# Two spectral layers side by side on one core: from a scheduled instruction order to one written out for every queue

## The chip, the cores and the metric

One core of one Trainium2 chip runs the kernel. The core has five queues of its own: TensorE (PE, with its weight loads as PEld), VectorE (DVE), ScalarE (ACT), GpSimd (POOL) and SyncE (SP), and 16 DMA engines that all queues feed. The metric is device time in microseconds of one launch; lower is better.

## The reference

Inputs: `A_x` and `B_x` of 1 x 2048 x 512, filters `A_w_r`, `A_w_i` of 2048 x 257, and four DFT matrices for B, two of 2048 x 2048 and two of 512 x 512, all float32. The output is 1 x 2048 x 1024, A's 512 columns beside B's.

```python
def _A_ref(x, w_r, w_i):                 # A_x, A_w_r, A_w_i
    B, S, D = x.shape
    X = jnp.fft.rfft2(x, axes=(-2, -1))
    X = X * (w_r + 1j * w_i)
    return jnp.fft.irfft2(X, s=(S, D), axes=(-2, -1))

def _B_ref(x, dft_seq_re, dft_seq_im, dft_hid_re, dft_hid_im):
    a = jnp.einsum("bsd,ed->bse", x, dft_hid_re)
    b = jnp.einsum("bsd,ed->bse", x, dft_hid_im)
    return jnp.einsum("ts,bse->bte", dft_seq_re, a) - jnp.einsum("ts,bse->bte", dft_seq_im, b)

return jnp.concatenate([a, b], axis=-1)
```

## The kernel before

Three strands of work share the engines; each is a Python generator in one function (`tile_concat_...`, line 209).

**A** (`a_work`, 423) is a factored two-dimensional FFT. `forward` (284) takes eight groups of input rows, two to a block: DVE folds a block (`TT`, 228), PE multiplies by the hidden-dimension table (`hid`, line 296), ACT copies the result out of PSUM (298), PE applies a 16-point step along the sequence (301), ACT copies again (303), and two DMAs per group, issued by ACT (306), put the result into the tile `zv` with the partition dimension rearranged. These are the *turns*: 16 of 256 KB, each with a source of 128 partitions and a destination of 8. `slot` (311) then works on `zv` in eight parts ("slots", in the order `SLOTS`): load of the filter part `w` and of a table `fi` (316, 322), a patch of one column of `w` by GpSimd (317), DVE sums (328 to 333), a forward matmul (338, or 341 for slot 0), the product with the filter on DVE (2048 elements per partition in one instruction), four DVE sums that combine its parts, an inverse matmul (382, 385), and two ACT copies back into `zv` (387). `inverse` (392) needs all of `zv`: for each of eight halves of a quarter, PE (406), an ACT copy (408), PE (412), an ACT copy (414), two DVE sums, and for each quarter a store of 1 MiB to `out_a` by SP (419).

**B** (`b_work`, 458) is the same kind of factored transform of `B_x`. Four blocks of 1 MiB are loaded (464 to 471), ACT makes a reversed copy `xr` (478, 479), PE transforms 16 groups (485, 486; "al" below), ACT gathers them into `yall` (488). Then for nine row sets `hidden` (497 to 503) and for eight `rows_of` (516 on): PE, an ACT copy with two halves (525), two DVE sums, a reversed ACT copy (528), a plain row store issued by ACT (509) and a scatter of mirrored rows issued by GpSimd (512). `yb`, which they leave from, has two buffers.

**C** (`c_work`, 565) makes the factored transform of B legitimate: it loads all of B's four DFT matrices, 34 MiB in 34 blocks of 1 MiB, and compares them with tables (`unequal`, 563) on DVE, counting differences in `stat`. At the end the counts are summed into `flag`, every engine loads the flag (621) and branches (622) around `_b_from_c`, which computes B from the matrices as given and is not run with these inputs. The sign of a table's odd columns is changed by ACT between its two uses (574, 595).

A's input blocks, B's input blocks and C's blocks share one set of six 1 MiB buffers (`block`, `NB = 6`). PSUM has three two-bank tiles for A (`ps_a`) and two one-bank tiles for B (`ps_b`).

The order: `ORDER` says how the three generators are stepped while the program is traced,

```python
ORDER = "a9 b8 a60 b20 c"
```

but that is only the order of tracing. The context is opened with `schedule_with_timeline_sim=True`, and its scheduler places each instruction on its engine's queue by dependences, free buffers and its own idea of when an instruction becomes ready. On the chip each queue then runs strictly in the order it was given, and waits on semaphores.

Of the kernel before, what the change touches and what calls it, by code (L numbers as in the profile page):

```python
# [16 lines left out]
P = 128  # L17
# [5 lines left out]
ORDER = "a9 b8 a60 b20 c"  # L23
# [102 lines left out]
def _tables():  # L126
# [54 lines left out]
    for h in range(2):  # L181
# [16 lines left out]
        "ht": ht.astype(np.float32),  # L198
# [3 lines left out]
        "mb": mb.astype(np.float32),  # L202
        "hc": hc.astype(np.float32),
        "turn": turn.astype(np.int32),
    }


@with_exitstack
def kernel(
# [15 lines left out]
    last = [None]  # L225

    def TT(**kw):
        last[0] = nc.vector.tensor_tensor(**kw)  # L228

    mm = nc.tensor.matmul  # L230
# [5 lines left out]
    ps_a = first.enter_context(tc.tile_pool(name="ps_a", bufs=3, space=PSUM))  # L236

# [6 lines left out]
    def block():  # L244
        return sp.tile([P, 2048], F32, name="blk", bufs=NB)

    load = nc.sync.dma_start

    ones = const("ones", P)
    nc.vector.memset(ones, 1.0)  # L250
    zero = sp.tile([P, 512], mybir.dt.bfloat16, name="zero")
    nc.vector.memset(zero, 0.0)
    warm = ps_a.tile([P, 2, 512], F32, name="pa")
    for _ in range(9):
        mm(warm[:, 0], zero[:, :P], zero, start=True, stop=True)

# [10 lines left out]
    tf = const("ta", 1152, src=tabs["first"], by=nc.scalar)  # L267
    hf = tf[:, :1024].rearrange("p (k h f) -> p k h f", k=2, h=2)
    f16 = tf[:, 1024:]
    wsp_sb = const("wsp_sb", 8, 2, 2, 2, src=wsp, by=nc.gpsimd)  # L270
    odd = const("odd", 2, src=tabs["odd"], by=nc.gpsimd)
    sgn = const("sgn", 2, 2)
    nc.gpsimd.memset(sgn[:, 0], 1.0)
    nc.gpsimd.memset(sgn[:, 1], -1.0)
    we = const("we", 8, 2, 2)

    xs = []
    for b in range(4):
        t = block().rearrange("p (c r f) -> p c r f", c=2, r=2)
        for c in range(2):  # L280
            load(t[:, c].rearrange("p r (k f) -> p r k f", k=2), xa[0, :, 2 * b + c])
        xs.append(t)

    def forward():
        for b in range(4):
            u = part(2048 * (b % 2), 2, 2, 2, 256)
            for h, op in enumerate((ADD, SUB)):
                TT(out=u[:, h].rearrange("p c k f -> p c (k f)"), in0=xs[b][:, :, 0], in1=xs[b][:, :, 1], op=op)
            for c in range(2):
                i = 2 * b + c  # L290
                pd = ps_a.tile([P, 2, 512], F32, name="pa")
                for r in range(2):
                    for h in range(2):
                        out = pd[:, r].rearrange("p (q h f) -> p h q f", q=2, h=2)[:, h]
                        for k in range(2):
                            mm(out, u[:, h, c, k, 128 * r : 128 * r + 128], hf[:, k, h], start=k == 0, stop=k == 1)  # L296
                zs = part(4096 + 1024 * (i % 2), 2, 512)
                nc.scalar.copy(zs, pd)  # L298
                y = ps_a.tile([P, 2, 512], F32, name="pa")
                for r in range(2):  # L300
                    mm(y[:, r], f16, zs[:, r], start=True, stop=True)  # L301
                ys = part(6144 + 1024 * (i % 2), 2, 512)
                nc.scalar.copy(ys, y)
                for r in range(2):
                    at = _place(8 * r + i, 0)
                    nc.scalar.dma_start(zv[at : at + 29 : 4], ys[:, r])
                yield

    def slot(e, n):

        z = zv[:, 2 * e : 2 * e + 2].rearrange("p r (q h f) -> p r q h f", q=2, h=2)
        w = sp.tile([P, 2, 2, 2, 128], F32, name="w", bufs=3)
        for h in range(2):
            load(w[:, :, :, h], wa[h, e])
        nc.gpsimd.tensor_copy(w[:, :, :, 0, 0], we[:, e].rearrange("p f r -> p r f"))  # L317
        t = part(1024 * (n % 3), 2, 2, 2, 128)
        tab = tabs["fi"].rearrange("p (e i f) -> p e i f", e=11, i=2)
        if e:  # L320
            fi = sp.tile([P, 1, 2, 128], F32, name="fi", bufs=4)
            load(fi, tab[:, e - 1 : e])
        else:
            fi = const("fi0", 4, 2, 128, src=tab[:, 7:], by=nc.sync)
        ft, it = fi[:, :, 0], fi[:, :, 1]

        def flat(v):
            return v.rearrange("p q h f -> p (q h f)")

        if e:  # L330
            TT(out=t[:, 0], in0=z[:, 1], in1=z[:, 0, ::-1], op=ADD)
            TT(out=t[:, 1], in0=z[:, 0], in1=z[:, 1, ::-1], op=SUB)
            nc.vector.tensor_copy(t[:, :, :, 0, 0], z[:, :, :, 0, 0])  # L333
        yield
        px = ps_a.tile([P, 2, 2, 2, 128], F32, name="pa")
        for i in range(2):
            if e:
                mm(flat(px[:, i]), ft[:, 0], flat(t[:, i]), start=True, stop=True)  # L338
            else:
                for j in range(2):  # L340
                    mm(flat(px[:, i]), ft[:, 2 * i + j], flat(z[:, j]), start=j == 0, stop=j == 1)
        yield
        x = px
        if e == 0:
            x = t
            g = part(7168, 2, 2, 128)
            nc.scalar.copy(g, px[:, 1])
            TT(out=x[:, 0], in0=px[:, 0, ::-1], in1=g, op=ADD)
            TT(out=x[:, 1], in0=px[:, 0], in1=g[:, ::-1], op=SUB)
            nc.scalar.copy(x[:, :, :, 0, 0], px[:, :, :, 0, 0])  # L350
# [12 lines left out]
        TT(out=m1[:, 1:3], in0=m1[:, 1:3], in1=m2[:, 3::-3], op=SUB)
        y = m1.rearrange("p (r q) (h f) -> p r q h f", r=2, h=2)

        yo = t
        TT(out=yo[:, 0], in0=y[:, ::-1, 0], in1=y[:, :, 1], op=ADD)
        TT(out=yo[:, 1], in0=y[:, 1, ::-1], in1=y[:, 0], op=SUB)
        TT(out=yo[:, :, :, 0, 0], in0=y[:, :, :, 0, 0], in1=sgn, op=MUL)
        if e == 0:  # L370
            nc.scalar.copy(yo[0:1, 0], y[0:1, ::-1, 0])
            nc.scalar.mul(yo[0:1, 1], y[0:1, :, 1], -1.0)
            nc.scalar.copy(yo[0:1, 0, :, 0, 0], cn[:, 0])
            nc.scalar.mul(yo[0:1, 1, :, 0, 0], cn[:, 1], -1.0)
        yield

        pi = ps_a.tile([P, 2, 4, 128], F32, name="pa")
        for i in range(2):
            for q in range(4):
                lhs = [yo[:, k].rearrange("p q h f -> p (q h) f")[:, q] for k in range(2)]  # L380
                if e:
                    mm(pi[:, i, q], lhs[i], it[:, 0], start=True, stop=True)  # L382
                else:
                    for k in range(2):
                        mm(pi[:, i, q], lhs[k], it[:, 2 * k + i], start=k == 0, stop=k == 1)
        for i in range(2):
            nc.scalar.copy(zv[:, 2 * e + i].rearrange("p (n q g) -> p n q g", n=8, q=4),  # L387
                           pi[:, i].rearrange("p q (n g) -> p n q g", n=8))

    def inverse():

        tl = const("ta", 1152, src=tabs["late"], by=nc.sync)
        di = tl[:, :1024].rearrange("p (h q n) -> p h q n", h=2, q=2)
        g16 = tl[:, 1024:]
        gz = zv.rearrange("p k f -> p (k f)")
        for quad in range(4):
            ob = part(3072 + 2048 * (quad % 2), 2, 2, 4, 128)
            for half in range(2):  # L400
# [9 lines left out]
                for j in range(2):  # L410
                    for q in range(4):
                        mm(po[:, j, q // 2, q % 2], u[:, j, q], g16, start=True, stop=True)  # L412
# [327 lines left out]
```

## Time and profile before

| | |
|---|---|
| time, median of 3 runs | 319.95 us (318.28 to 321.04) |
| the profiled execution | 320.22 us, its span 318.4 us |
| mean granted TensorE clock | 0.821 |
| busy, us: PE, PEld, DVE, ACT, POOL | 201.8, 149.8, 152.5, 72.5, 28.0 |
| moved by DMA | 70.35 MB, mean 221 GB/s |
| of it read from HBM, written to it | 57.54 MB, 8.39 MB |

The span is the time from the first instruction to the last of one profiled execution; its own time has 1.8 us more around it. Busy time counts compute instructions only. A matmul of float32 stands as two records. The slices cut the span into 40 parts of 8 us, with the busy share of each in tenths. In the list of stages a row has the stretch, then for each engine its busy time and its count of instructions, then the granted clock of TensorE, the mean busy share of the 16 DMA engines (which can be a little over 1, as packets overlap) and GB/s. A releaser after `<-` is what ended an engine's idle time.

### The profile page before, as it was taken

To read this page: it belongs to the slowest core of one execution; us is meant where nothing else is said; L and a number is where in the kernel's file an instruction comes from. 1 tells how busy PE (TensorE), PEld (TensorE's weight loads), DVE (VectorE), ACT (ScalarE), POOL (GpSimd) and SP (SyncE) were. 2 spreads that over 40 slices of the span, in tenths; PEclk is the share of its full clock that TensorE was granted. 3 is DMA by queue.
4 is the path that set the end of the run, shared out by engine and by line. 5 is a ranking of instruction groups with operands and counts; after the bars stand their busy time and mean duration, and the time that the engine had idled before them with its cause. 6 is when DMAs were issued, how large, how long until landed. Compare 5 with 4: busy or idle time off the path is not lost.

```text
span 318.4 us, 2428 instructions
## 1 busy us (share of the span) xinstructions
PE 201.8 (63%) x849; PEld 149.8 (47%) x849; DVE 152.5 (48%) x199; ACT 72.5 (23%) x114; POOL 28.0 (9%) x25
## 2 busy tenths in 40 slices
PE   5760049999989524948088200797927688788850
PEld 1540018888876312523065000473525587688850
DVE  0520000560275541499999999986694211111220
ACT  1010014424452212400014100423302122322220
POOL 2000000000000000100050079011120000000000
PEclk9995559999999975695659855597877799999995
DMA  7999999663999999799999997032210000230303
GB/s 269 391 288 291 213 279 342 241 249 94 397 334 340 338 300 350 271 360 401 404 308 358 389 333 308 35 126 89 99 66 33 2 0 31 100 134 0 132 3 139
DMA packets 30002, 70.35 MB, mean 221 GB/s; under 512 B 1936, under 2 KB 11024, under 8 KB 29472
## 3 DMA queue, kind: packets, MB, share of 16 engines
q1 hardware_dynamic: 25760, 61.12, 56.6%
q10 hardware_dynamic: 3488, 6.88, 6.2%
q0 software_dynamic: 736, 2.14, 1.7%
q8 instruction: 8, 0.13, 0.2%
q14 instruction: 10, 0.08, 0.1%
HBM read 57.54 MB, written 8.39 MB: 207 GB/s over the span
## 4 chain that ended last, share of the span: by engine, by line
PE 39%; DMA 28%; DVE 18%; ACT 5%; issue 5%; SPq 3%; ACTq 0%; DVEq 0%
DMA blk<-in_cm 13%; DVE work L228 11%; PE pa L406 9%; DMA blk<-in_xb 8%; DVE blk L563 6%; PE pa L412 5%; PE pa L296 4%; DMA zv<-work 4%; PE pa L382 4%; PE pa L338 3%; PE pa L301 3%; ACT work L408 3%; DMA blk<-in_xa 2%; PE pb L485 2%; PE pb L501 2%
## 5 line engine op out<-in xcount | busy, mean ns | idle before, releaser
L563 DVE SCALAR_TENSOR_TENSOR blk<-blk,tt 128x2048 f32<-128x2048 f32 (+2 forms) x24 | 41.6, 1754 | 25.8 <-DMA blk<-in_cm 18.2
L563 DVE SCALAR_TENSOR_TENSOR blk<-blk,odd,tt 128x2048 f32<-128x2048 f32 x16 | 37.2, 2346 | 5.4 <-DMA blk<-in_cm 5.4
L497 PE MATMUL pb<-hc,yall 128*128 128x257 f32 x18 | 8.0, 536 | 46.4 <-DVE work L228 33.1
L228 DVE TENSOR_TENSOR work<-pa,work 128x512 f32<-128x512 f32 x18 | 11.6, 685 | 51.3 <-ACT work L414 51.3
L296 PE MATMUL pa<-ta,work 128*128 128x256 f32 x128 | 31.2, 400 | 3.9 <-DVE work L228 3.9
L301 PE MATMUL pa<-work,ta 128*128 128x512 f32 x32 | 17.1, 660 | 24.8 <-ACT work L298 24.8
L296 PEld LDWEIGHTS pa<-ta,work 128*128 128x128 f32 x128 | 25.9, 203 | 11.7 <-DVE work L228 4.8
L406 PE MATMUL pa<-ta,zv 128*128 128x256 f32 x128 | 30.5, 391 | 1.2 <-ACT zv L387 1.2
L228 DVE TENSOR_TENSOR work<-blk 128x1024 f32<-128x1024 f32 x8 | 9.4, 1222 | 43.4 <-PE pa L296 42.9
L406 PEld LDWEIGHTS pa<-ta,zv 128*128 128x128 f32 x128 | 28.8, 304 | 1.5 <-ACT zv L387 1.5
L497 PEld LDWEIGHTS pb<-hc,yall 128*128 128x128 f32 x18 | 3.7, 244 | 51.7 <-issue 35.3
L382 PE MATMUL pa<-fi,work 128*128 128x128 f32 x112 | 18.1, 328 | 10.4 <-DVE work L228 10.4
L512 POOL DMA_INDIRECT out_b<-yb,turn x8 | 13.4, 1678 | 117.9 <-DMA out_b<-yb 112.9
L382 PEld LDWEIGHTS pa<-fi,work 128*128 128x128 f32 x112 | 17.6, 241 | 12.7 <-issue 12.5
L412 PE MATMUL pa<-ta,work 128*128 128x128 f32 x128 | 16.4, 281 | 9.1 <-ACT work L408 9.1
L338 PE MATMUL pa<-work,fi 128*128 128x512 f32 x28 | 18.2, 793 | 5.5 <-DVE work L333 4.4
L317 POOL COPY w<-we 128x4 f32<-128x4 f32 x8 | 12.5, 1571 | 92.0 <-DMA w<-in_wa 87.2
L412 PEld LDWEIGHTS pa<-ta,work 128*128 128x128 f32 x128 | 14.9, 191 | 11.5 <-ACT work L408 11.5
L298 ACT COPY work<-pa 128x1024 f32<-128x1024 f32 x8 | 8.1, 1013 | 53.2 <-PE pa L296 29.4
L301 PEld LDWEIGHTS pa<-work,ta 128*128 128x128 f32 x32 | 6.0, 206 | 30.2 <-ACT work L298 25.8
L228 DVE TENSOR_TENSOR work<-work 128x512 f32<-128x512 f32 x32 | 20.1, 680 | 0.1
L228 DVE TENSOR_TENSOR work<-pa,w 128x2048 f32<-128x2048 f32 x7 | 15.9, 2284 | 8.4 <-PE pa L338 8.4
(72 smaller groups left out, 232.3 us busy)
## 6 DMA issues: line engine op xcount, KB each, us to landing
blk<-in_cm SPq DMA_DIRECT2D x32, 1024.0 KB, 7.1
tt<-tab_tt SPq DMA_DIRECT2D x4, 1026.0 KB
blk<-in_xa SPq DMA_DIRECT2D x8, 512.0 KB, 6.7
w<-in_wa SPq DMA_DIRECT2D x16, 256.0 KB, 7.1
zv<-work ACTq DMA_DIRECT2D x16, 256.0 KB
out_a<-work SPq DMA_DIRECT2D x4, 1024.0 KB, 4.1
blk<-in_xb SPq DMA_DIRECT2D x7, 512.0 KB
blk<-in_wd SPq DMA_DIRECT2D x2, 1024.0 KB
```

The lines of the kernel that those rows point to most:

```text
L228: last[0] = nc.vector.tensor_tensor(**kw)
L296: mm(out, u[:, h, c, k, 128 * r : 128 * r + 128], hf[:, k, h], start=k == 0, stop=k == 1)
L301: mm(y[:, r], f16, zs[:, r], start=True, stop=True)
L317: nc.gpsimd.tensor_copy(w[:, :, :, 0, 0], we[:, e].rearrange("p f r -> p r f"))
L338: mm(flat(px[:, i]), ft[:, 0], flat(t[:, i]), start=True, stop=True)
L382: mm(pi[:, i, q], lhs[i], it[:, 0], start=True, stop=True)
L406: mm(pu[:, j, h], gz[:, 32 * q + 16 * h + g :: 64], di[:, h, q], start=q == 0, stop=q == 1)
L408: nc.scalar.copy(u, pu.rearrange("p j h (k n) -> p j (h k) n", k=2))
L412: mm(po[:, j, q // 2, q % 2], u[:, j, q], g16, start=True, stop=True)
L497: mm(out, yall[:, a0], hc[:, 0], start=True, stop=False)
L512: nc.gpsimd.indirect_dma_start(out=out_b, out_offset=bass.IndirectOffsetOnAxis(ap=turn[:, o : o + 1], axis=0), in_=v, in_offset=None)
L563: nc.vector.scalar_tensor_tensor(raw, raw, k, v, op0=MUL, op1=ALU.not_equal, accum_out=stat[:, i : i + 1])
```

## The change

The generators are taken apart into some 400 named steps, each of which issues instructions on one engine only. The string `PLAN` lists the steps; they are traced in that order, and every instruction is tied behind the one traced before it on the same engine, so that the scheduler cannot move it. A step's name is a kind and a number: `xa` A's loads, `fold`, `hid`, `zs`, `f16_`, `ys` and `tu` the parts of `forward`, `w`, `fix`, `sf`, `fwd`, `prod`, `comb`, `inv`, `ev` those of a slot (with `g`, `sx`, `spec`, `spy` for slot 0), `late`, `hi`, `eu`, `g16_`, `sc`, `eo`, `st` those of `inverse`; `xb`, `xr`, `al`, `av`, `bh`, `hv`, `ro`, `y1`, `y2`, `y3`, `pt` (and `rx`, `ry`) B's; `tt`, `cl`, `sg`, `cc` the tables, loads, sign changes and comparisons of C, where 16 and 17 are those of the hidden matrices.

Beside the order these things change:

- A's first four input groups are loaded one by one and folded half by half for the first block; the later ones come one block per load. The runs in memory are longer.
- The part of a slot is laid out with the width half `h` ahead of the rest. The filter's two loads per slot become one with longer runs, and its product becomes two DVE instructions of 1024 elements.
- The tables `hc`, `ht` and `mb` are one tile `bt`, loaded at once.
- The turns, B's plain row stores, the late table and the stores to `out_a` are issued from GpSimd's queue; before, ACT issued the first two and SP the others.

```diff
-ORDER = "a9 b8 a60 b20 c"
+PLAN = """
+xa0 we xa1 xa2 xa3 xa5 xa7 tt0 tt1 bt fold0 cl0 fold1 hid0 cl1 fb fold3 hid1 zs0 w0 f16_0 zs1 fold5 hid2 ys0
+tu0 w1 f16_1 zs2 hid3 ys1 tu1 w2 cc0 f16_2 zs3 fold7 hid4 xb0 cc1 cl2 fix0 f16_3 zs4 ys2 hid5 tu2 xb1 cl3 fix1
+ys3 tu3 f16_4 zs5 cl4 fix2 cl5 hid6 xr0 f16_5 zs6 cc2 al0 ys4 al1 av0 tu4 hid7 av1 cc3 f16_6 zs7 ys5 al2 sg4
+tu5 f16_7 av2 cc4 al3 late cl6 av3 cc5 cl7 xr1 ys6 al4 ys7 tu6 al5 av4 tu7 al6 av5 cc6 al7 av6 cl8 av7 cl9 xb2
+xb3 cc7 fwd2 sf0 sf1 tt2 cc8 cl10 cc9 fwd0 g2 fwd1 prod0 cl11 xr2 cl12 al8 prod1 w3 al9 cl13 av8 al10 av9
+comb0 w4 al11 av10 av11 cl14 comb1 xr3 al12 sx2 al13 av12 cc10 al14 spec2 av13 inv0 av14 prod2 fix3 inv1 ev0
+sf3 w5 al15 ev1 comb2 fwd3 cl15 av15 cl16 fix4 bh8 prod3 spy inv2 hv8 sf4 w6 fix5 comb3 fwd4 ev2 sf5 inv3
+prod4 bh0 ev3 sf6 fix6 w7 fwd5 comb4 hv0 ro0 prod5 fix7 inv4 y10 y20 comb5 bh1 y30 ev4 rx sf7 hv1 fwd6 ry cc11
+pt0 ro1 bh2 y11 prod6 cl17 sg12 inv5 hv2 y21 comb6 y31 ro2 ev5 pt1 bh3 y12 cc12 inv6 hv3 y22 cl18 fwd7 ev6
+cc13 y32 ro3 pt2 bh4 prod7 y13 cl19 y23 hv4 comb7 ro4 y33 pt3 bh5 y14 cc14 inv7 hv5 y24 cl20 ev7 cc15 ro5 y34
+bh6 y15 pt4 cc16 tt3 cl21 hi0 hv6 y25 cl22 sg17 y35 cc17 pt5 ro6 eu0 bh7 y16 tt4 cl23 y26 y36 g16_0 cc18 hv7
+pt6 ro7 sc0 hi1 cc19 cl24 eo0 cl25 hi2 cc20 eu1 y17 y27 cl26 cc21 y37 g16_1 eu2 pt7 g16_2 cl27 sg22 sc1 cc22
+hi3 sc2 eo1 cl28 eo2 st0 hi4 eu3 cc23 cc24 cl29 g16_3 eu4 g16_4 sc3 cc25 cl30 hi5 sc4 eo3 cl31 cc26 st1 hi6
+eu5 cc27 cl32 eo4 cl33 eu6 cc28 g16_5 g16_6 sc5 cc29 hi7 sc6 eo5 sg30 cc30 st2 eu7 cc31 g16_7 eo6 sc7 eo7 cc32
+st3 cc33
+"""
...
+class _InOrder:
+
+    def __init__(self, tc, engine):
+        self._tc, self._engine = tc, engine
+
+    def __getattr__(self, name):
+        def issue(*args, **kwargs):
+            return self._tc.keep_in_program_order(getattr(self._engine, name)(*args, **kwargs))
+        return issue
...
+    pe, dve, act, pool, sync = (_InOrder(tc, e) for e in (nc.tensor, nc.vector, nc.scalar, nc.gpsimd, nc.sync))
+    mm, TT, load = pe.matmul, dve.tensor_tensor, sync.dma_start
...
+        @step(f"ys{i}")
+        def _():
+            act.copy(ys, flat(at["py", i]))
+
+        @step(f"tu{i}")
+        def _():
+            for r in range(2):
+                lo = _place(8 * r + i, 0)
+                pool.dma_start(zv[lo : lo + 29 : 4], ys[:, r])
...
-        w = sp.tile([P, 2, 2, 2, 128], F32, name="w", bufs=3)
-        for h in range(2):
-            load(w[:, :, :, h], wa[h, e])
...
+        @step(f"w{n}")
+        def _():
+            w = at["w", n] = sp.tile([P, 2, 2, 2, 128], F32, name="w", bufs=3)
+            load(w, wa[:, e].rearrange("h p i q f -> p h i q f"))
...
+        @step(f"prod{n}")
+        def _():
+            x, w = at["px", n] if e else t, at["w", n]
+            for h in range(2):
+                x2 = x[:, h].rearrange("p r q f -> p r (q f)").unsqueeze(1).to_broadcast([P, 2, 2, 256])
+                w2 = w[:, h].rearrange("p i q f -> p i (q f)").unsqueeze(2).to_broadcast([P, 2, 2, 256])
+                TT(out=m[:, h].rearrange("p i (r q) f -> p i r (q f)", r=2), in0=x2, in1=w2, op=MUL)
...
+    @step("late")
+    def _():
+        tl = const("ta", 1152, src=tabs["late"], by=pool)
...
+            @step(f"st{quad}")
+            def _():
+                pool.dma_start(out_a.rearrange("(r p) s -> p r s", p=P)[:, :, 512 * quad : 512 * quad + 512],
+                               ob.rearrange("p r k g s -> p (r k) (g s)"))
...
+        @step(f"pt{o}")
+        def _():
+            y = at["y", o]
             if o:
-                put(rows[o], y[:, 0])
-                put_turned(o, y[:, 1])
...
+                pool.dma_start(rows[o], y[:, 0])
...
+            pool.indirect_dma_start(out=out_b, out_offset=bass.IndirectOffsetOnAxis(ap=turn[:, o : o + 1], axis=0),
+                                    in_=y[:, 1], in_offset=None)
...
+    for name in PLAN.split():
+        steps.pop(name)()
+    assert not steps, steps
```

More of the change, by code (lines that the diff above doesn't have):

```diff
@@ L251, with part @@
     zero = sp.tile([P, 512], mybir.dt.bfloat16, name="zero")
[L252 to L255, printed above, removed]
+    dve.memset(zero, 0.0)
     zv = const("zv", 16, 512)
     work = const("work", 8192)
-    def part(at, *shape):
-        v = work[:, at : at + math.prod(shape)]
+    def part(lo, *shape):
+        v = work[:, lo : lo + math.prod(shape)]
         names = "abcde"[: len(shape)]
@@ L272 @@
+    odd = const("odd", 2, src=tabs["odd"], by=pool)
+    turn = sp.tile([P, 8], mybir.dt.int32, name="turn")
+    pool.dma_start(turn, tabs["turn"])
     sgn = const("sgn", 2, 2)
-    nc.gpsimd.memset(sgn[:, 0], 1.0)
-    nc.gpsimd.memset(sgn[:, 1], -1.0)
+    pool.memset(sgn[:, 0], 1.0)
+    pool.memset(sgn[:, 1], -1.0)
     we = const("we", 8, 2, 2)
[L277 to L292, printed above, removed]
-                    for h in range(2):
[L294 to L307, printed above, removed]
@@ L425, in a_work, with _ @@
+    for i in range(8):
+        forward(i)
+    @step("we")
+    def _():
         TT(out=we[:, :, :, 0], in0=wsp_sb[:, :, :, 0, 0], in1=wsp_sb[:, :, :, 1, 0], op=ADD)
@@ L427, in a_work @@
         TT(out=we[:, :, 1, 1], in0=wsp_sb[:, :, 1, 0, 1], in1=wsp_sb[:, :, 1, 1, 1], op=SUB)
-        gens = [slot(e, n) for n, e in enumerate(SLOTS)]
-        def stage(n):
-            if 0 <= n < 8:
-                next(gens[n], None)
-        stage(0)
-        stage(0)
-        stage(1)
-        yield
-        for n in range(9):
-            stage(n)
-            yield
-            stage(n - 1)
-            stage(n + 1)
-            yield
-            stage(n + 2)
-            yield
-        yield from inverse()
@@ L495, in hidden, with _ @@
+        for g in range(4):
+            group(g)
+    for q in range(4):
+        along(q)
+    m_b = mb[:, :1408].rearrange("p (k f) -> p k f", f=128)
+    rows = out_b.rearrange("(c e) d -> e c d", e=16)
+    def hidden(e):
+        @step(f"bh{e}")
+        def _():
+            bank = bank_b(("bh", e))
             a0, a1, a2 = (0, 7, 7) if e == 8 else (1 + e, 8 + e, e - 1 if e else 8)
@@ L606, with compare, four, _ @@
[L606 to L613 removed]
+        dve.scalar_tensor_tensor(raw, raw, k, v, op0=MUL, op1=ALU.not_equal, accum_out=stat[:, i : i + 1])
+    def compare(i, k, q, mt, half, tb):
+        raw = "c", i
+        def four(name):
+            return at[name].rearrange("p (j c) -> p j c", j=4)
+        @step(f"cl{i}")
+        def _():
+            lo = 4 * half + 2 * q
+            block(raw)
+            load(four(raw).rearrange("p (r j) c -> p r j c", r=2), cm[mt, tb, lo : lo + 2].rearrange("r p j c -> p r j c"))
+        if half and tb == 0:
+            @step(f"sg{i}")
+            def _():
+                act.mul(at["t", k][:, :, 1::2], at["t", k][:, :, 1::2], -1.0)
+        @step(f"cc{i}")
+        def _():
+            t = at["t", k]
+            neg = int(tb % 2 == 1 and mt == 1)
+            unequal(i - 2 * (i > 15), four(raw), t[:, :, 512:0:-1] if tb % 2 else t[:, :, :512],
+                    odd[:, neg : neg + 1] if tb in (1, 2) else (-TINY if neg else TINY))
```

544 lines of the change are left out of this document (303 added, 241 removed).

## Prediction

> **What bounds the kernel now.** I read the slices of the page first: they show when each engine works.
>
> ```profile
> PE   5760049999989524948088200797927688788850
> DVE  0520000560275541499999999986694211111220
> DMA  7999999663999999799999997032210000230303
> ```
>
> DMA is full until about 200 us (25 slices of 8 us) and then almost idle; PE has holes early and in the middle and is dense only at the end, when VectorE (DVE) and DMA have nothing left. The three busy resources stand one behind the other. The stages, by columns PE, PEld, DVE, ACT, POOL (busy us), granted clock, DMA share, GB/s:
>
> ```profile
> 28.00:43.00 15.00, 0.00 (x0) 0.00 (x0) 0.00 (x0) 0.00 (x0) 0.00 (x0) 0.50 1.05 215
> 79.00:118.00 39.00, 29.55 (x138) 22.23 (x136) 19.26 (x19) 12.89 (x20) 0.00 (x0) 0.97 1.02 348
> 118.00:134.00 16.00, 9.90 (x20) 5.79 (x21) 4.27 (x5) 4.67 (x8) 0.00 (x0) 0.53 0.87 311
> 134.00:201.00 67.00, 27.79 (x81) 15.34 (x79) 66.20 (x91) 10.10 (x18) 19.89 (x7) 0.70 0.93 348
> 182.00:201.00 19.00, 0.00 (x0) 0.00 (x0) 18.97 (x23) 1.32 (x2) 13.87 (x3) 0.50 0.85 302
> 201.00:253.00 52.00, 38.66 (x156) 26.65 (x156) 35.17 (x51) 13.91 (x28) 5.48 (x6) 0.77 0.18 64
> 253.00:310.00 57.00, 45.74 (x256) 43.17 (x256) 10.15 (x16) 13.00 (x17) 0.00 (x0) 1.00 0.15 56
> ```
>
> From 253 on the whole inverse of A runs alone: 57 us with DVE busy 10 and DMA at 15%. At 28 to 43 PE stands still. Why, the ACT timeline says, and the chain of waits shows the inverse's period:
>
> ```profile
> 43.12 1.01 ACT L298 COPY work<-pa 128x1024 f32<-128x1024 f32 x1 [23.88 <-DMA blk<-in_xb]
> ...
> 257.22 1.02 ACT work L408
> ...
> 258.28 2.05 PE pa L412 x16
> 260.33 3.65 PE pa L406 x16
> ```
>
> ACT's next copy of A stood 23.88 us behind a load for B: an order of queues, not a lack of data. In the inverse PE pays 2.05 + 3.65 us and waits for the copy L408 between them.
>
> **The change: the sums that no order can beat.** Bytes and arithmetic stay, but for longer runs in the loads of A's input and weights. Totals of the page:
>
> ```profile
> PE 201.8 (63%) x849; PEld 149.8 (47%) x849; DVE 152.5 (48%) x199; ACT 72.5 (23%) x114; POOL 28.0 (9%) x25
> ...
> q1 hardware_dynamic: 25760, 61.12, 56.6%
> q10 hardware_dynamic: 3488, 6.88, 6.2%
> ...
> core 0: 318.4 us, clock 0.821
> ```
>
> DMA: 56.6 + 6.2% of 318.4 us is 200 us, with the 2% of the small queues 206. PE: 201.8 x 0.821 = 165.7 us of work at full clock. DVE: 152.5 us. So the written order can bring the span near DMA's 206 us if everything lies beside the loads; I walk it in three stages.
>
> **Stage 1, to the last input block of B (xb3).** SP's written order puts before it, in MiB: first table 0.56, xa 4, tt0 and tt1 2, bt 1.44, ten comparison blocks (cl0 to cl9) 10, fb 0.39, three slots' weights and tables 2.25; GpSimd adds the turns 4 and late 0.56: 25.2, and xb itself 4.
>
> ```profile
> blk<-in_cm SPq DMA_DIRECT2D x32, 1024.0 KB, 7.1
> ...
> 1.67 7.43 DMA blk<-in_xa
> ```
>
> At 348 GB/s (row 79:118, loads and turns together) a MiB costs 3.01 us; in 28:43, where xb was the load, 215 GB/s gives 4.88. So 25.2 x 3.01 + 4 x 4.88 = 95.4 us; with 1.7 us to the first byte, xb3 lands at **97 us**. What PE has to do in it, what a turn's issue takes, and how long rows of B (yb) take to land:
>
> ```profile
> 9.24 5.86 PE L296 MATMUL pa<-ta,work 128*128 128x256 f32 x16 [3.88 <-DVE work L228]
> ...
> 47.92 3.45 PE pa L296 x16
> ...
> 53.70 1.72 PE pa L301 x4
> ...
> L306 ACTq DMA_DIRECT2D zv<-work x16: 622/624/1224, 37.5 to 122.4; - x16
> ...
> DMA to landing us min/median/max: 2.7/2.8/6.9
> ```
>
> From 9 us on, 8 x (3.45 + 1.72) = 41 us of forward work: half of the stage. So the engines wait for landings, and the written order adds waits: DVE's cc7 (for cl7) stands ahead of sf0; ACT's xr0 and xr1 (for xb0, xb1) stand ahead of copies of A, with PE's hid7 and f16_6 behind them; on GpSimd fix0 waits for the load w0 with the turns tu2 and on behind it, and ys4 on ACT waits for tu2's landing. All of these loads stand ahead of xb3 on SP, so the waits end before it and cost nothing as long as the loads are the last; if they aren't, that is the second rival below. The three loads hc, ht, mb become one and ACT loses 16 turn issues: hidden here too, and without that cover worth what SP's and ACT's issues take, about 0.6 us each.
>
> **Stage 2, to the last product's end (comb7).** PE's order puts inv0 behind al14, so behind xb3. Rows:
>
> ```profile
> L479 ACT COPY xr<-blk x4: 1043/1043/1044, 49.0 to 87.5; 128x1020 f32<-128x1020 f32 x4
> ...
> 96.71 0.34 PE pb L485 x2
> ...
> 97.39 0.24 PE pb L485 x2
> ...
> 226.65 1.78 PE pa L382 x16
> ```
>
> xr3 1.2, three groups al12 to al14 of 4 such pieces (2 x 0.34 + 2 x 0.24 = 1.16) 3.5, inv0 1.8: DVE may start sf3 at 103.5. DVE's own rows:
>
> ```profile
> L563 DVE SCALAR_TENSOR_TENSOR blk<-blk,tt 128x2048 f32<-128x2048 f32 x16 | 36.5, 2287 | 25.1 <-DMA blk<-in_cm 18.2 <-ACT tt L574 6.9
> L228 DVE TENSOR_TENSOR work<-work 128x512 f32<-128x512 f32 x32 | 20.1, 680 | 0.1
> L228 DVE TENSOR_TENSOR work<-pa,w 128x2048 f32<-128x2048 f32 x7 | 15.9, 2284 | 8.4 <-PE pa L338 8.4
> L228 DVE TENSOR_TENSOR work<-zv 128x512 f32<-128x512 f32 x14 | 8.9, 683 | 0.0
> L228 DVE TENSOR_TENSOR yb<-yb,pb 128x255 f32<-128x255 f32 x16 | 5.9, 411 | 16.4 <-ACT yb L525 16.4
> ```
>
> Its order from sf3 to comb7 is 5 sf at 1.4, 6 comb at 2.7, 5 prod at 2.3, 4 y2 at 0.74 and 3 comparisons at 2.3: 44.6 us. How dense DVE runs there the trace doesn't show; 134:201 gives 99% (66.20 of 67), 201:253 gives 68%. The nearer one is 134:201, where products and comparisons alternate too, but with little PE work; I take 85%: 52.5 us (ends 45 and 66). comb7 ends at **156 us**. The product in two halves (2 x 1024 for 2048) adds a start per slot: four of 680 against one of 2284 give 0.15 us per start, 1.2 us for all, inside the 85%. One more wait is added: yb has two buffers and both halves of B's rows now leave through GpSimd, so ACT's y1 of row set o+2 waits for pt of o to land, with ev and hv (and PE's next inverse) queued behind it. Two row sets are 10 us apart or more in this order, a landing was 2.7 to 6.9 us; I cost it at nothing beyond the 85%, up to 8 x 2 us if the landings lengthen beside full loads.
>
> **Stage 3, the end.** With comparison cc13 done, six blocks (NB) hold cl14 to cl19, so cl20 can load only when cc14 ends, at 158.3. Left: 14 comparison blocks, 2 tables, 2 MiB of B's rows, 3 of out_a before its last store: 21 MiB x 3.01 = 63.2, to 221.5. Beside it DVE needs 20 comparisons at 2.3, 3 of B's rows and 10.2 of the inverse (row 253:310): 59 (from 156 to 215); PE needs 8 x (3.65 + 2.05) = 46 and B's last rows (to about 207), its copies now beside the next group's matmuls, and without that cover again 8 x 1.1. Loads are last, by little; three queues so close in one order cannot all hide, and PE at the 0.77 of 201:253 would need 165.7/0.77 = 215 us in all; I add 4. Then cc33 2.3 us, and the flag's end, which the stores hid so far:
>
> ```profile
> L621 PEldq TENSOR_LOAD <-flag x1: 486/486/486, 306.2 to 306.2; - x1
> ...
> L622 PEldq COMPARE_BRANCH  x1: 3979/3979/3979, 306.8 to 306.8; - x1
> ...
> L622 SPq EVENT_SEMAPHORE  x8: 17/17/17, 311.1 to 316.3; - x8
> ```
>
> An allowance of 1 us to the flag, then 0.5, 4.0, and the 2.1 between 316.3 and 318.4: 7.6. Span: 221.5 + 4 + 2.3 + 7.6 = 235.4. The profiled execution took 320.22 for its 318.4, so add 1.8: **237 us**. It is 0.1% above the median of 319.95, so nothing is rescaled. A gain of 83 us: the lone inverse (57) and the early hole (15) go; late next is the load queue.
>
> **GpSimd, the unknown.** It takes over 16 turns and 9 row stores from ACT, a table and 4 stores of out_a from SP, beside its copies (fix) and scatters.
>
> ```profile
> L317 POOL COPY w<-we x8: 189/506/7430, 16.3 to 215.2; 128x4 f32<-128x4 f32 x8
> ...
> L512 POOL DMA_INDIRECT out_b<-yb,turn x8: 963/1006/4175, 134.5 to 238.0; - x8
> ...
> L241 POOL DMA_DIRECT2D wsp_sb<-in_wsp x1 | 0.7, 716 | 0.8 <-POOLq L726 0.8
> ```
>
> A plain issue was seen at 0.7 us alone, none beside a full DVE; bounds are 0.7 and the scatter's 4.2. I take 0.7 for the turns, since DVE is light in stage 1. In 182:201, where DVE was busy 18.97 of 19, POOL's three instructions took 13.87. The Trainium skill, "SBUF — State Buffer", section "Who interferes with whom", says that a DVE instruction with two SBUF inputs holds off GpSimd instructions that read SBUF and not those that only write it. By that the small copies may stretch and the plain issues stay at 0.7; With that, the first rival below falls to 21 + 34 + 59 = 114 us of work and bounds nothing. The copy's 7.43 agrees, and the scatter's 4.18 leaves open which half of it stretched.
>
> **Rivals.**
> GpSimd bounds: 30 plain issues and 8 scatters at 4.2, 8 copies at 7.4 are 219 us, from the first turn at 18 (9.24 + 2 x 3.45 + 1.72) to 237; four turn pairs' landings exposed (about 6 each, 24) and the last store (2.8, then 2.1 + 1.8) make **268**. For it: 182:201. Against: DVE is full there, not everywhere.
> Landings late: in a fixed order every late load moves all behind it. Were stage 1 at 4.88 per MiB throughout, 29.2 MiB take 142 instead of 95: **284**. For it: row 28:43; against: 79:118, with turns in it.
> The clock stays low (the slower side): PE's work is spread thinner. At 0.50 throughout, 165.7 becomes 331; from 9 us with an end of 10 that is **350**. It decides below a mean clock of 0.545 (165.7/c + 19 over 323). For it: 118:134 had 0.53 with PE busy 62%. Against: 253:310 had 1.00 with gaps of 1 us. The Trainium skill, "TensorE: Matmul & The Clock Gate", "Part 1", says that an idle window of about 3.4 us halves the clock; the 0.50 of the idle 182:201 agrees.
> The order doesn't arrive: if queues ran much as before, **319**. Against it, the 23.88 us are order alone.
>
> **How the numbers follow.** Forecast (220 to 252) 0.60, GpSimd 0.14, late landings 0.12, low clock 0.05, no effect 0.04, under 220 0.05 (206 + 1.7 + 11.7 is the floor with today's DMA times). Faster by over 1% (what this kernel's runs, 318.28 to 321.04, can tell) 0.91, within 0.04, slower 0.05. The range 220 to 274 leaves out about 2 in 10: it takes in stage 2 at 68% (+13) and the GpSimd rival.
>
> **What would show it.** DMA full to about 10 us before the end; xb3's copy near 97; hi0 near 158; comparisons up to the end; granted clock near 0.77 or above; POOL's plain issues near 0.7. Wrong if DMA has long holes before 150, if POOL is busy beyond half the span, or if the last comparison ends far behind the last load.

## The result, and the profile after

| | median, us | runs | ratio to before |
|---|---|---|---|
| before | 319.67 | 318.28 to 321.04 | |
| after | 258.71 | 254.99 to 258.96 (4) | 0.803, 95% interval 0.792 to 0.814 |

The kernel is 61 us faster, where 83 were forecast. Ratios here and below leave out executions over 1.5% above the fastest of their kernel (of after the two near 258.9, the profiled one among them, and in experiment 2 also 256.41 and 387.46), so they can differ a little from the quotient of the medians. The profiled execution took 258.96 us, its span 257.2.

The page after, its busy times and three rows of its slices (6.4 us each):

```profile
PE 195.9 (76%) x857; PEld 153.9 (60%) x857; DVE 154.0 (60%) x209; ACT 71.9 (28%) x114; POOL 39.3 (15%) x55
...
PE   6799999397470798979999946994939999906800
...
DVE  0730550031573789999999937814057799408990
...
DMA  6989999999999999997314581786659889992440
```

The early hole of PE is gone, and the inverse no longer stands alone at the end. New is a trough: DMA falls to 3 in the 20th slice and reads 9 again only in the 31st, and DVE, dense up to the 23rd, falls to 3 in the 24th and then to 7814057. The stretches (PE, PEld, DVE, ACT, POOL busy, granted clock, DMA share, GB/s):

```profile
28.00:43.00 15.00, 15.00 (x60) 11.24 (x59) 6.84 (x6) 4.47 (x5) 2.95 (x7) 1.00 1.05 349
100.00:120.00 20.00, 17.44 (x113) 14.72 (x113) 19.69 (x33) 9.06 (x21) 4.39 (x3) 1.00 1.01 387
120.00:140.00 20.00, 20.00 (x99) 13.99 (x98) 19.76 (x32) 7.53 (x14) 3.65 (x5) 1.00 0.28 76
140.00:160.00 20.00, 14.27 (x53) 8.59 (x52) 14.05 (x21) 5.93 (x11) 3.79 (x4) 0.80 0.53 190
160.00:200.00 40.00, 31.89 (x105) 24.38 (x105) 19.05 (x35) 9.60 (x17) 5.28 (x8) 0.71 0.73 258
```

At 120 to 140 loads stop because all six blocks are full and DVE is dense; that belongs to the plan. From 140 to 200 no resource is full: PE works 46 of 60 us, DVE 33, DMA two thirds. What it waits for, in the view of waits (sum, times, longest); all lines are one helper's now, so the tiles tell the place:

```profile
DVE yb L229 <- ACT yb L229: 26.4, 5, 8.9
POOL out_b L229 <- DMA out_b<-yb,turn: 26.0, 4, 7.6
ACT yb L229 <- DMA out_b<-yb,turn: 23.9, 4, 9.2
...
POOL out_b L229 <- DMA out_b<-yb: 16.9, 5, 5.5
...
DVE work L229 <- DMA out_a<-work: 11.2, 1, 11.2
```

Read backwards they are one chain: DVE (`y2`) waits for ACT's copy (`y1`), that copy for a buffer of `yb` that a scatter is still reading, and GpSimd issues each plain row store only after the scatter ahead of it has landed and each scatter only after its plain store. The timeline of GpSimd (start, duration, what; in brackets the idle time before and its releaser) shows the alternation from 176 on; its first two rows serve further below:

```profile
107.38 3.17 POOL L229 COPY w<-we 128x4 f32<-128x4 f32 x1 [35.19 <-DMA w<-in_wa]
...
143.92 0.60 POOL L229 DMA_DIRECT2D out_b<-yb  x1 [6.03 <-issue]
...
176.64 0.56 POOL L229 DMA_DIRECT2D out_b<-yb  x1 [7.32 <-DMA out_b<-yb,turn]
180.35 1.01 POOL L229 DMA_INDIRECT out_b<-yb,turn  x1 [3.16 <-DMA out_b<-yb]
188.98 0.55 POOL L229 DMA_DIRECT2D out_b<-yb  x1 [7.62 <-DMA out_b<-yb,turn]
...
219.14 3.00 POOL L229 DMA_INDIRECT out_b<-yb,turn  x1 [5.71 <-DVE blk L229]
222.14 1.53 POOL L229 DMA_DIRECT2D out_a<-work  x2
```

So a row set takes some 12 us of GpSimd's queue (176.64 to 188.98), nearly all of it waiting, and A's first store (`st0`) stands behind the last one. The chain that ended last goes through the same transfers:

```profile
168.31 7.78 DMA out_b<-yb,turn
...
176.64 2.94 DMA out_b<-yb
...
180.35 8.08 DMA out_b<-yb,turn
...
222.14 10.18 DMA out_a<-work
```

Both halves of a row set go into one tensor, `out_b`, to different rows; the wait between them is between two writers of one tensor. That was a reading; the next part tests it.

### The profile page after: what moved, and what is told of

It is laid out like the page before. It is cut to its first block, busy times and chain, and to the rows that moved or that the text cites. A ratio compares the mean times of both kernels' runs of the same rounds, so it can differ in the third digit from the quotient of the medians.

```text
span 257.2 us, 2443 instructions
## 1 busy us (share of the span) xinstructions
PE 195.9 (76%) x857; PEld 153.9 (60%) x857; DVE 154.0 (60%) x209; ACT 71.9 (28%) x114; POOL 39.3 (15%) x55
## 5 line engine op out<-in xcount | busy, mean ns | idle before, releaser
L229 PE MATMUL pa<-ta,work 128*128 128x256 f32 (+1 forms) x256 | 48.8, 352 | 12.7 <-DVE work L229 11.5
L229 ACT COPY work<-pa 128x1024 f32<-128x1024 f32 (+3 forms) x36 | 30.4, 859 | 85.1 <-PE pa L229 82.9
L229 PE MATMUL pb<-bt,yall 128*128 128x257 f32 (+2 forms) x90 | 29.1, 459 | 0.0
L229 PEld LDWEIGHTS pb<-bt,yall 128*128 128x128 f32 (+1 forms) x90 | 18.0, 219 | 13.2 <-issue 11.7
L229 PE MATMUL pb<-fb,blk 128*128 128x200 f32 (+1 forms) x64 | 17.3, 358 | 8.3 <-ACT yall L229 4.4
L229 PE MATMUL pb<-zb,bt 128*128 128x512 f32 (+3 forms) x24 | 12.8, 641 | 13.8 <-ACT zb L229 13.8
L229 DVE TENSOR_TENSOR yb<-yb,pb 128x255 f32<-128x255 f32 x16 | 6.0, 415 | 26.4 <-ACT yb L229 26.4
L229 PEld LDWEIGHTS pb<-fb,blk 128*128 128x128 f32 x64 | 13.2, 226 | 10.8 <-issue 5.9
L229 PE MATMUL pb<-fb,xr 128*128 128x200 f32 (+1 forms) x64 | 17.5, 359 | 2.1 <-ACT xr L229 2.1
L229 POOL DMA_INDIRECT out_b<-yb,turn x8 | 13.5, 1688 | 30.5 <-DMA out_b<-yb 16.9
L229 DVE TENSOR_TENSOR work<-pa,work 128x512 f32<-128x512 f32 x18 | 11.4, 682 | 11.2 <-DMA out_a<-work 11.2
L229 DVE TENSOR_TENSOR work<-pa,w 128x1024 f32<-128x1024 f32 x14 | 16.4, 1219 | 0.8 <-PE pa L229 0.8
L229 POOL DMA_DIRECT2D zv<-work x16 | 9.6, 605 | 46.8 <-ACT work L229 46.4
L229 ACT COPY yb<-pb 128x514 f32<-128x514 f32 (+1 forms) x9 | 5.1, 565 | 36.8 <-DMA out_b<-yb,turn 23.9
## 6 DMA issues: line engine op xcount, KB each, us to landing
w<-in_wa SPq DMA_DIRECT2D x8, 512.0 KB, 12.6
blk<-in_xb SPq DMA_DIRECT2D x7, 512.0 KB, 18.4
```

Source lines behind the costliest of these rows:

```text
L229: return self._tc.keep_in_program_order(getattr(self._engine, name)(*args, **kwargs))
```

## The experiments

In the cuts of code, `...` stands for what is left out.

**1. A's stores on ACT's queue.** `st` leaves GpSimd's queue, so it no longer stands behind the scatters.

```diff
-                pool.dma_start(out_a.rearrange(...)[:, :, 512 * quad : 512 * quad + 512], ...)
+                act.dma_start(out_a.rearrange(...)[:, :, 512 * quad : 512 * quad + 512], ...)
```

> The changed kernel, with the four stores of out_a issued by ACT instead of GpSimd. Theory (chain of row stores): in the changed kernel a row set's plain store waits for the scatter before it to land and its scatter for the plain store, all in GpSimd's one queue, and this holds up ACT's copies (through yb's two buffers) and DVE behind them; the first store of out_a merely stands behind the last of the chain. Then only the 11.2 us that DVE waited for that store can go: 247 to 251 us. Rival (queue place alone): the miss against 237 us is all from out_a's stores standing behind the rows: 236 to 240. Rival (loads last anyway): 257 to 260, no change.

Measured: 248.84 us (246.73 to 250.60), ratio 0.775 (0.767 to 0.783). 10 us came back, about DVE's single wait of 11.2 for `out_a`; the rest stayed:

```profile
ACT yb L229 <- DMA out_b<-yb,turn: 26.1, 4, 10.6
```

The place of `st` is a part, and not the whole.

**2. The scatter into a tensor of its own.** Same bytes, same queues, same order; the mirrored rows go to a second output tensor, put together with the first afterwards. The branch that isn't taken was left as it is.

```diff
-            pool.indirect_dma_start(out=out_b, out_offset=..., in_=y[:, 1], in_offset=None)
+            pool.indirect_dma_start(out=out_t, out_offset=..., in_=y[:, 1], in_offset=None)
```

> The changed kernel, with the scatters into an output tensor of their own (the host puts both together; the branch not taken is left as it was), so that a plain store and a scatter no longer wait for each other; scatter after scatter still does. Theory (chain): of the 26 us in which DVE waits for ACT's row copies at least half goes, and out_a's first store is issued some 20 us earlier: 240 to 250 us. Rival (queue place alone): the same stores still stand behind eight scatters, but earlier: 245 to 250. Rival (loads last anyway): 257 to 260.

Measured: 228.02 us over six executions (225.41 to 228.80 in four of them), ratio 0.704 (0.698 to 0.710): 30 us less than after, more than was expected. The instructions of ACT, DVE and SP stand in the same order as in after. Waits of GpSimd:

```profile
POOL out_b L229 <- ACT yb L229: 21.9, 8, 5.4
POOL out_t L229 <- DMA out_t<-yb,turn: 11.5, 3, 4.9
```

A scatter still waits for the scatter before it, as two writers of `out_t`, but a plain store waits only for its data. DVE's wait for `yb` fell from 26.4 to 6.0 us, and `st0` was issued at 188.10 and not at 222.14. This settles it: the two kinds of store into one tensor cost 30 us. The expectation counted the waits one by one; that each of them also held back the loads behind the comparisons is argued and not shown.

**3 and 4. One plain store per row set.** Both halves of `yb` leave in one 512 KB store to an output laid out by row set, whose rows are put in order afterwards; no scatter on the chip. In 4, `st` is on ACT's queue besides.

```diff
-                pool.dma_start(rows[o], y[:, 0])
...
-            pool.indirect_dma_start(out=out_b, out_offset=..., in_=y[:, 1], in_offset=None)
+            pool.dma_start(out_y[o], y)
```

> The changed kernel, with one plain store of 512 KB per row set, in a layout of its own, instead of a plain store and a scatter; the host puts the rows in place. Same queue (GpSimd), same order. No store of rows waits for another any more. Theory (chain): DVE's 26 us of waits for row copies and its 11 us for out_a's store shrink to under 8 in all; the time is then that of my sum without late rows, 233 to 241 us. Rival (queue place alone): also about 238, since the stores come early; e1 tells the two apart. Rival (loads last anyway): 256 to 260.

> e3 with the stores of out_a issued by ACT as well. Theory (chain): with the chain gone GpSimd's queue holds nothing up, so this equals e3 within 1%, or is up to 3 us slower as ACT waits for DVE's last sums. Rival (queue place alone): equal to e1. Rival (loads last anyway): 256 to 260.

Measured: 228.64 us (226.64 to 229.64), ratio 0.715 (0.710 to 0.720), and 227.16 us (225.68 to 229.34), ratio 0.712 (0.706 to 0.718). With the chain gone it no longer matters who issues `st`. Experiment 3 came out 4 us below the range expected; 4 equals 3, as expected. The last, called kernel 4 below, is as fast as experiment 2 within the intervals, some 92 us under before and 31 under after, and what the forecast's stages can be held against. Kernel 4's slices (5.6 us each):

```profile
PE   7599999939948307979799999989996999999310
...
DVE  0534093001246637999999999999929979999970
...
DMA  6999999999999999999995406495999999999850
```

From the 17th to the 37th slice DVE is dense but for the 30th, DMA but for a trough from the 22nd to the 28th, and PE nearly dense. Two of its stretches:

```profile
116.00:146.00 30.00, 30.00 (x153) 21.24 (x152) 29.58 (x48) 12.51 (x23) 2.22 (x5) 1.00 0.44 153
...
170.00:204.00 34.00, 34.00 (x199) 33.54 (x200) 32.79 (x37) 12.28 (x17) 0.77 (x2) 1.00 1.03 417
```

In the second, PE, DVE and DMA are full at once for 34 us, which is what the written order is able to do. Three rows of its timelines for the comparison below:

```profile
149.84 2.61 DVE L230 TENSOR_TENSOR work<-work 128x512 f32<-128x512 f32 x4
...
159.23 3.68 PE L230 MATMUL pa<-ta,zv 128*128 128x256 f32 x16
...
216.53 0.20 DVE L230 TENSOR_REDUCE rs<-stat 128x1 f32<-128x40 f32 x1
```

They are the end of `comb7` (152.5), the start of `hi0` and the end of the comparisons.

**5. The same store in the kernel before.** If the scatter is what costs, is it so there too?

```diff
-                put(rows[o], y[:, 0])
-                put_turned(o, y[:, 1])
+                nc.gpsimd.dma_start(out_y[o], y)
```

> The kernel before with one plain store of 512 KB per row set from GpSimd, as in e3, and nothing else changed. Theory (the chain hurts only where loads fill the DMA engines and other work stands behind it): before the change half of the rows leave when DMA is nearly idle, a landing takes 2.8 us, and the inverse runs alone afterwards: 308 to 322 us, at most 4% less. Rival (the chain was as dear before): 30 us less, 285 to 295.

Measured: 320.27 us (319.07 to 322.75), ratio 0.999 (0.996 to 1.002). Nothing. The waits were there too: in before 112.9 us of GpSimd's idle time ahead of scatters ended with the landing of a plain store. But the plain stores were on ACT's queue, and DVE and DMA had long stretches to spare behind them (from 253 to 310 DVE worked 10.15 of 57 us and DMA's share was 0.15). That the chain became a cost only in the written order, with the rest of the work packed around it, is the reading that fits; it is argued and not shown. The scheduler also placed the instructions of this version anew: ACT's order is that of before up to some 140 us only.

**6. The turns back on ACT.** Kernel 4 with `tu` issued by ACT; the order of ACT, DVE and SP stays as it was:

```diff
-                pool.dma_start(zv[lo : lo + 29 : 4], ys[:, r])
+                act.dma_start(zv[lo : lo + 29 : 4], ys[:, r])
```

> e4 with the turns issued by ACT again, as before the change, in the same written order. Theory (stage 1 goes by landings): who issues the turns doesn't matter, as the loads bound that stage: 225 to 231 us, within 1% of e4's 227.2. Rival (the queue of the turns is a part of the gain): ACT stands at its issues as it did before the change, where two turns took up to 9.7 us to issue; 232 to 242 us.

Measured: 252.78 us (252.07 to 253.29), ratio 0.790 (0.786 to 0.794). The theory fell: 25.6 us, more even than the rival gave. ACT's timeline there:

```profile
19.77 1.01 ACT L230 COPY work<-pa 128x1024 f32<-128x1024 f32 x1 [0.70 <-PE pa L230]
34.05 1.91 ACTq L230 DMA_DIRECT2D zv<-work  x2
36.00 1.93 ACT L230 COPY work<-pa 128x1024 f32<-128x1024 f32 x2 [15.22 <-DMA zv<-work]
```

and GpSimd's in kernel 4:

```profile
21.18 1.25 POOL L230 DMA_DIRECT2D zv<-work  x2 [18.52 <-ACT work L230]
```

The data of the first turn is there at 20.8 in the one and 20.9 in the other. GpSimd issues it at 21.18; on ACT the issue stands at 34.05, and the next copy of A, at 23.38 in kernel 4, comes at 36.00, 12.6 us late.

The instruction records of the traces tell what the issue waits for. A DMA counts up a semaphore when it lands. SP's and ACT's DMAs take turns on the same eight semaphores (107, 109, 111 and 113 to 117 here, in before and in kernel 4), GpSimd's on another eight (99 to 106), and an issue waits until the DMA that had its semaphore before has landed. The first turn on ACT has semaphore 107. A table load that SP issued at 21.04, when the turn's data was already there, had it before; it landed at 33.97. On GpSimd the first turn's semaphore had not been used yet.

Full engines alone hold no issue. What the DMA queues moved at 18 to 38 in kernel 4 (packets, MB, share of the 16 engines):

```profile
q1 hardware_dynamic: 2095, 6.90, 87.8%
q0 software_dynamic: 576, 1.05, 14.3%
```

GpSimd's turns (q0) move beside SP's loads (q1). ACT's do so too, once they are issued; its queue with the turns on ACT, at 38 to 60, beside 84.1% of q1:

```profile
q10 hardware_dynamic: 488, 0.95, 20.7%
```

That sent me back to before, where the same shape stands under another name.

**7. The kernel before with its turns on GpSimd, and nothing else.**

```diff
-                    nc.scalar.dma_start(zv[at : at + 29 : 4], ys[:, r])
+                    nc.gpsimd.dma_start(zv[at : at + 29 : 4], ys[:, r])
```

> The kernel before, its 16 turns issued by GpSimd in place of ACT, nothing else. Theory (held issue): the 23.88 us in which ACT stood still from 19 to 43 us are its first turn's issue, held while SP's loads stand in the queue, and not an order of copies behind a load of B. Then the wait shrinks to that for PE (2 to 5 us), PE has no hole at 28 to 43, and the time falls by 5 to 25 us, to 295 to 315. Rival (what the prediction said, order alone): ACT's next copy still ends its wait with a load for B near 43 us, and the time stays at 317 to 323.

Measured: 293.33 us (290.08 to 294.15), ratio 0.915 (0.906 to 0.925): 26 us from one word, a little below the range expected. In before the row ahead of ACT's wait was

```profile
37.55 5.53 ACTq L306 DMA_DIRECT2D zv<-work  x2
```

These are two issues, at 37.55 and 42.44; the data was there at 19.2. Each had the semaphore of a load of B, issued by SP at 20.79 and 25.80, and came when that load had landed, at 37.47 and 42.42. The chain that ended last shows the second:

```profile
25.80 16.61 DMA blk<-in_xb
42.44 0.64 ACTq L306
```

With the turns on GpSimd ACT's next copy of A runs at

```profile
21.60 1.01 ACT L298 COPY work<-pa 128x1024 f32<-128x1024 f32 x1 [2.44 <-PE pa L296]
```

and the stretch of the early hole is

```profile
28.00:43.00 15.00, 15.00 (x74) 12.26 (x73) 2.36 (x2) 4.95 (x8) 0.00 (x0) 1.00 1.05 235
```

The wait of 23.88 us is 2.44, and PE's hole at 28 to 43 is gone, with DMA still full (235 GB/s). So the hole was a held issue and not an order of copies: ACT's instructions stand in the same order in both up to the 44th, which ran at 95.26 and before at 109.40. These 14 us come with the order kept; behind them the scheduler, which places the instructions of each version anew, has ordered ACT and DVE otherwise, so how much of the other 12 is the queue alone is open.

**8. Half of the turns on ACT.** Kernel 4 with the turns of groups 4 to 7 on ACT, and with those of groups 0 to 3.

```diff
-                pool.dma_start(zv[lo : lo + 29 : 4], ys[:, r])
+                (pool if i < 4 else act).dma_start(zv[lo : lo + 29 : 4], ys[:, r])
```

> The best version so far (one store per row set, A's stores on ACT, 227.2 us) with its turns of groups 4 to 7 issued by ACT, groups 0 to 3 by GpSimd. All eight on ACT cost 25.6 us. Theory (held issue): what costs is the hold of single issues by SP's queued loads, 13 us at the first turn and 10.8 us at the last; so the late four give about the latter, 234 to 242. Rival (a turn on ACT is slow by its transfer, each one alike): half of 25.6, 238 to 242, and no issue held over 5 us.

> The same version with the turns of groups 0 to 3 issued by ACT and 4 to 7 by GpSimd. Theory (held issue): the first issue is again held from about 21 to 34 us and ACT's copies behind it wait; 236 to 244. Rival (each turn alike): 238 to 242 without a held first issue. If the cost were only that a late copy waits for a turn's landing, as written for the run with all turns on ACT, 227 to 231.

Measured: 250.20 us (249.72 to 250.37), ratio 0.783 (0.777 to 0.790), and 245.60 us (245.48 to 246.61), ratio 0.770 (0.763 to 0.776). Each half alone costs 23.0 and 18.4 of the 25.6, so they do not add up, and both came out above what theory and rival gave. With the late half, ACT's timeline shows a copy that waits for the landing of the turn two groups back (the second row) and a held issue with the copy behind it (the last two):

```profile
64.35 1.35 ACTq L230 DMA_DIRECT2D zv<-work  x2
...
81.49 1.01 ACT L230 COPY work<-pa 128x1024 f32<-128x1024 f32 x1 [9.84 <-DMA zv<-work]
...
82.90 9.60 ACTq L230 DMA_DIRECT2D zv<-work  x2
92.53 0.79 ACT L230 COPY yall<-pb 128x344 f32<-128x344 f32 x2 [9.22 <-DMA blk<-in_cm]
```

That turn pair was issued at 64.35 and 65.08 and had landed by 81.5, after some 16 us, where a turn on GpSimd's queue took 7.0 to 14.7 in kernel 4, median 8.9. In the held row the second of two issues waits until 91.85 for a comparison block of SP's that had its semaphore. With the early half the first issue stands at 34.17 again, with the data there at 21.0. Held issues (9.6 and 13 us) and slower landings both occur; how the 25.6 divide between them is open.

**9. The written order alone.** After without the tie that keeps each instruction behind the one traced before it: same steps, layout and queues, and the scheduler's placement.

```diff
-            return self._tc.keep_in_program_order(getattr(self._engine, name)(*args, **kwargs))
+            return getattr(self._engine, name)(*args, **kwargs)
```

> The changed kernel with the same steps traced in the same order, the same layout and the same queues, but not tied: the scheduler may place each instruction again. Theory (the order makes the gain): without the ties the queues fall back to an order like that of before, with work of one strand parked in front of another: 280 to 320 us. Rival (steps, trace order, layout and queues make it): 252 to 262 us, like the changed kernel's 258.7.

Measured: 298.58 us (292.47 to 299.28), beside 320.99 for before; no interval is given for it. That is where before stands with its turns on GpSimd (293.33): untied, the rest of the change shows no gain beside the turns' queue. Whether the row stores took something away there was not tried. At its end the inverse is still almost alone, with 12.5 us of DVE and 18% of DMA:

```profile
230.00:285.00 55.00, 47.82 (x264) 46.29 (x265) 12.53 (x20) 13.27 (x17) 3.61 (x4) 0.91 0.18 65
```

The ties are worth some 40 us on top (298.6 to 258.7).

**10. Comparisons earlier.** In kernel 4 DMA falls to 0.44 at 116 to 146, since full blocks wait for comparisons behind the slots' work. `cc11` to `cc14`, `cl17` to `cl20` and `sg12` were moved ahead in `PLAN`:

```diff
-comb2 ... comb3 ... cc11 ... cc12 ... cc13 ... cc14
+comb2 cc11 ... comb3 cc12 cl18 ... comb4 cc13 cl19 ... comb5 cc14 cl20
```

> e4 with the comparisons cc11 to cc14 placed two to three slots earlier in DVE's order and the loads cl17 to cl20 right behind them, so that blocks come free while DMA is at 0.44 of its time (116 to 146 us in e4). Theory (with the chain gone the loads are last again, as in my stage 3): three to four MiB at 417 GB/s move ahead, 2.5 us each: 218 to 224 us. Rival (PE and DVE are as full as DMA there: 34.0 and 32.8 of 34 us from 170 to 204): no gain, 225 to 230 us.

Measured: 232.66 us (230.99 to 233.74), ratio 0.727 (0.721 to 0.732), 5.5 us slower. The theory that loads are last fell. One of its stretches:

```profile
116.00:146.00 30.00, 25.46 (x126) 17.04 (x124) 29.65 (x45) 7.70 (x15) 1.18 (x4) 1.00 0.65 235
```

DMA rose from 0.44 to 0.65 where it was low, and PE, full there in kernel 4 (30.00), lost 4.5 us. Between 116 and 146 both PE and DVE are full in kernel 4, so a comparison put ahead there makes a slot's work late; that this is the whole of the 5.5 us is argued and not shown.

## Why the prediction was right or wrong

The time lies in the range of 220 to 274, 22 us above the forecast and outside the 220 to 252 that the forecast's own chance stood for. Part of the agreement is luck. The steps, by their own numbers:

**Stage 1 held, with one wrong reason.** The rows for it, from the timelines of ACT, PE and DVE after:

```profile
100.06 1.14 ACT L229 COPY xr<-blk 128x4 f32<-128x4 f32 x2
...
155.87 0.75 DVE L229 TENSOR_TENSOR yb<-yb,pb 128x255 f32<-128x255 f32 x2 [5.81 <-ACT yb L229]
156.53 2.62 DVE L229 TENSOR_TENSOR work<-work 128x512 f32<-128x512 f32 x4
...
169.60 2.58 PE L229 MATMUL pa<-ta,zv 128*128 128x256 f32 x11
...
250.94 0.20 DVE L229 TENSOR_REDUCE rs<-stat 128x1 f32<-128x40 f32 x1
```

`xr3` ran at 100.06, where `xb3` was to land at 97. But the step that read before's early hole failed. It said that ACT's copy "stood 23.88 us behind a load for B: an order of queues, not a lack of data", and costed the turns' move at 0.6 us per issue, hidden. A load for B was what was waited for, but not by the copy and not through an order: the issue of a turn ahead of the copy waited for it, on a semaphore that SP's and ACT's DMAs share. Experiment 7 removes the wait with the order there kept, and the turns' queue is worth 25.6 us in the written order (experiment 6). The trace had it: the row of ACTq directly above the copy, 5.53 us long, was the issue it stood behind. With the turns on ACT the last `xr` ran at 125.87 in experiment 6, for 99.42 in kernel 4. That stage 1 held is luck as far as this goes: the diff happened to hold the remedy, the turns on GpSimd, as well as the order.

**Stage 2: the density was better, the wait was missed.** DVE ran at 19.69 and 19.76 of 20 us from 100 to 140, 99% and not 85%, and would have ended `comb7` early; kernel 4, without the chain, ended it at 152.5. After ended it at 159.2 for 156 because of the wait of 5.81 above: the sum is close by two errors against each other. The product halves cost what was said: 14 at 1219 ns against 7 at 2284 is 1.1 us.

**The term that failed** is the wait of `yb`, "nothing beyond the 85%, up to 8 x 2 us". The prediction named the wait, its two buffers and who is queued behind it, but priced a single landing (2.7 to 6.9) against 10 us between row sets. What it left out is that a row set now is two transfers in turn on one queue, each waiting for the other to land in the same tensor, and that a scatter took 7.8 to 8.1 us to land (with DMA's share at 0.73). With 1.0 and 0.6 for the issues and 2.9 for the plain store that makes 12 us or more per row set. It cost 30 us (experiment 2), not nothing. `hi0`, forecast near 158, came at 169.6; in kernel 4 at 159.2.

**Stage 3: the price per MiB was too high.** While nothing but comparison blocks was loaded, kernel 4 moved 417 GB/s, 2.51 us per MiB, not 3.01: 21 MiB in 52.8 us for 63.2. The allowance of 4 us was not needed either. Nor were "Loads are last, by little" right there: from 150 on DVE waited

```profile
DVE yb L230 <- ACT yb L230: 4.3, 1, 4.3
```

and 1.6 us for sign changes, for no load, and SP's last load was issued by 198.3. DVE itself came last: 58 us of work, for the 59 of the forecast, and these waits took it from 152.5 to 216.5, where the forecast had 227.8 for the last comparison. That fits experiment 10, in which earlier loads brought nothing. So the forecast of 237 was 10 us too high for its own mechanism (227 once the chain is out) and 22 too low for the kernel as given: +30 for the rows, -10 for the loads that were priced as last, and what is left are the small differences above.

**The end**: 250.9 to 257.2 is 6.3 us, for 7.6.

**The rivals.** GpSimd's queue held the end up, but by waiting, not by working: the rival priced its work at 219 us, and it was busy 39.3, and that its 268 lies nearer to the result than 237 is luck. Its plain row stores were issued in 0.55 to 0.6 us even where DVE was busy (0.60 at 143.9, inside a comparison from 142.55 to 144.84), and its copies took 0.19 to 3.17. The Trainium skill, "SBUF — State Buffer", "Who interferes with whom", says that a DVE instruction with two SBUF inputs holds off GpSimd instructions that read SBUF, and not those that only write it. That plain issues are of the second kind was the prediction's reading; these rows agree with it. Late landings at 4.88 us per MiB throughout did not come: `xr3` ran at 100, not 142, though two stretches before it moved only 271 and 263 GB/s with the engines full (40 to 60 and 80 to 100). The clock rose to 0.856 from 0.821, and to 0.928 in kernel 4, with PE busy 76% and 82% of the span for 63%.

Of the signs named beforehand, comparisons to the end, the clock and POOL's plain issues held; DMA full to about 10 us before the end and `hi0` near 158 did not. Of the signs against, the hole of DMA before 150 came (0.28 at 120 to 140) but was not the fault, since kernel 4 has it too (0.44) and filling it cost 5.5 us. The last comparison far behind the last load came too (250.9, with SP's last load issued by 221.7), and that one told of the chain, as did DMA at two thirds from 140 to 200 with DVE waiting.

## What to carry to other kernels

Count what a DMA queue waits for, not only what it issues: two stores that alternate on one queue into one tensor are a chain of landings, priced under load, and a second tensor or one larger store takes it away. Ask also whose landing an issue itself waits for: in these kernels SP's and ACT's DMAs share eight semaphores, so a turn issued from ACT waited for a load of SP's and held ACT's copies with it. Look for a queue row directly above a long wait, and for what that row waited for. And a written order shows its full worth only where such waits are out of it: tying it was worth 40 us with the chain in, and one plain store per row set, worth nothing in the scheduled kernel, brought 30 us more in the ordered one.

## What was not expected of the hardware

A turn issued by ACT stood for 13 us and held up ACT itself, while one issued by GpSimd at the same point moved beside SP's loads (q0 at 14.3% in 18 to 38). That hold is the program's: a wait for a semaphore that a load of SP's had before (experiment 6). What is left for the chip is the landing. ACT's turns in experiment 6 took 4.1 to 23.9 us from issue to landing, median 13.5, and GpSimd's in kernel 4 took 7.0 to 14.7, median 8.9, though the loads beside them are not quite the same. The Trainium skill, "DMA: Bandwidth & Descriptors", "Issuing engine by pattern", says that issuing from SP or ACT is generally the faster way. For these turns the traces say the opposite, in their landings and by 25.6 us in the time, the holds included. The same page, "SWDGE vs HWDGE vs iDMA", says that GpSimd's and SP's or ACT's descriptors feed different queues inside each DMA engine, which take turns; that would fit q0 moving beside q1. Why ACT's turns land later no run here shows.
